# Low weights for all 128 rows in the last matmul of each spatial group

## The chip, the cores and the metric

The kernel runs on one core of a Trainium2 chip. The metric is device time in microseconds (us) of one execution on that core. Three runs were timed; the median counts.

## What is computed

The reference chains three blocks in float32: a causal windowed attention (4 batches, 8 heads, 576 positions, head size 64), a mixing block with a hidden layer of 2048, and a gated block. The change lies in the last one:

```python
h = np.maximum(x @ w_in, 0.0)
u, v = (h[..., :d_ff // 2], h[..., d_ff // 2:])
mu = np.mean(v, axis=-1, keepdims=True)
var = np.mean((v - mu) ** 2, axis=-1, keepdims=True)
v_n = (v - mu) / np.sqrt(var + 1e-06)
v_s = np.einsum('ts,bsd->btd', w_spatial, v_n) + b_spatial[None, :, None]
gated = u * v_s
return (gated @ w_out).astype(np.float32)
```

Here `x` is 4 x 576 x 512, `h` has 1024 columns (512 for `u`, 512 for `v`) and `w_spatial` is 576 x 576. The product with `w_spatial` runs over the 576 positions `s`.

## The kernel before

All matmuls of the two later blocks take float32 operands split in two: a high part that TensorE (PE) reads as float32r, and a low part, the float32 value less the high part. A product a·b is summed from three matmuls: high·high, high·low and low·high. ScalarE (ACT) makes a high part by a copy, GpSimd (POOL) or VectorE (DVE) the low part by a subtraction.

The order of every engine's work comes from a planner (class `Plan`). Each operation is added with an engine, an estimated cost, what it reads and writes, and a priority; `run` simulates the engines with these costs and emits the operations in the order in which they would start. So a changed cost or an added operation can reorder other work on any engine.

The gated block goes batch by batch (`b` = 0 to 3), in three stages each, with one more between:

- `values_of` multiplies by the v half of `w_in`, for chunks of 128 positions, and normalises each position. Per chunk DVE gets mean and variance, POOL the power -1/2 (tile `rs`, L831), DVE the normalised values (L833), ACT the high part (L848) and DVE the low part (L851).
- `outputs_of` of the batch before multiplies by `w_out`.
- `gates_of` first makes the u half (its matmuls are recorded at L779 to L781, those of the helper `triple`), then the **spatial product**.

576 positions are 64 + 4 x 128. The four chunks of 128 (`c` = 1 to 4) have separate tiles for high and low. The first 64 positions (`c` = 0) are packed: in one tile of 128 partitions, one half of the rows holds the high part and the other half the low part of the same 64 positions. For even batches the high part is in rows 0 to 63, for odd batches in rows 64 to 127 (L841 and L843 write the two halves; slice `hi` in `gates_of` names the half with the high part). The transposed spatial weights `ws[0]` of these 64 positions are therefore loaded twice, into both halves of a tile; `ws[c][:, 0]` is the high and `ws[c][:, 1]` the low part (L759 ACT, L761 POOL).

For each batch the spatial product has 8 groups: 4 blocks of 128 columns times 2 halves of 288 positions. One group is 14 matmuls into one PSUM tile (function `spatial`, L881 to L891):

- for each of the four chunks three matmuls, L886 high·high, L887 high·low, L888 low·high, each 128 rows by 288 columns;
- L890: the packed tile against the high weights in all 128 rows, which gives high·high and low·high together;
- L891: the packed tile against the low weights, in the 64 rows of the high part alone.

After a group DVE adds the bias (L897) and multiplies by the u half (L899), ACT takes high parts (L910) and POOL low parts (L912). The groups' results go to eight PSUM tiles in turn (names `acc`, `sc`, `f`, `at`).

Of the kernel before, what the change touches and what calls it, by code (L numbers as in the profile page):

```python
# [11 lines left out]
F32 = mybir.dt.float32  # L12
F32R = mybir.dt.float32r
# [3 lines left out]
ALU = mybir.AluOpType  # L17
PSUM = bass.MemoryType.PSUM

B, H, S, D = 4, 8, 576, 64  # L20
# [45 lines left out]
def f32(ap):  # L66
    return ap.bitcast(F32)
# [171 lines left out]
def mm(n, m=128):  # L239
    return (max(n, 2 * m) + m / 4) / 2400  # L240


def dve(n):
    return n / 960 + 0.066
# [6 lines left out]
def act(n, src=0.06, aps=0):  # L251
    return n / 1200 + src + 0.09 * aps


def pool_tt(n):
    return 0.0021 * n + 0.15
# [3 lines left out]
def tile_kernel(ctx, tc, qT, kT, v, U, V, w1, w2, w_in, wspT, bsp, w_out, bias, out):  # L260
    nc = tc.nc
    ctx.enter_context(nc.allow_low_precision("operands split exactly into float32r parts"))
    P = Plan()
# [432 lines left out]
    for pair in range(4):  # L696
        P.dma(128, 192, lambda pair=pair: nc.sync.dma_start(out=bias_t[:, pair], in_=bias[:, pair]),
              w=[bias_t.part(pair)], prio=20 * pair + 0.5)
# [24 lines left out]
    def late(tag, n):  # L723
        return Ring(late_pool, tag, n, [end_att])
# [6 lines left out]
    base = 2e4  # L731
# [19 lines left out]
    ws = []  # L751
    for c, (s0, n) in enumerate(CH):
        st = r_raw.new([128, S], F32)

        b_ = (r_wb if c < 4 else r_raw).new([128, 2, S], F32R)
        for p0 in (0, 64) if c == 0 else (0,):
            P.dma(n, S, lambda st=st, p0=p0, s0=s0, n=n: nc.sync.dma_start(
                out=st[p0 : p0 + n], in_=wspT[s0 : s0 + n, :]), w=[st], prio=base - 900)
        P.add("ACT", act(S, 0.09), lambda st=st, b_=b_: nc.scalar.copy(out=b_[:, 0], in_=st.ap()),  # L759
              r=[st], w=[b_.part(0)], prio=base - 900)  # L760
        P.add("POOL", pool_tt(S), lambda st=st, b_=b_: nc.gpsimd.tensor_tensor(  # L761
            out=b_[:, 1], in0=st.ap(), in1=f32(b_[:, 0]), op=ALU.subtract), r=[st, b_.part(0)], w=[b_.part(1)], prio=base - 900)
        ws.append(b_)
    bb = late("bb", 1).new([128, S], F32)
    P.dma(128, S, lambda: nc.sync.dma_start(
        out=bb.ap(), in_=bsp.rearrange("(o s) -> o s", o=1).broadcast_to([128, S])), w=[bb], prio=base - 1000)
# [5 lines left out]
    def next_ps(shape):  # L772
        turn[0] += 1
        return pss[turn[0] % 8].new(shape, F32)

    def triple(o, pairs):

        for i, (lh, ll, rh, rl) in enumerate(pairs):
            nc.tensor.matmul(o, lh, rh, start=i == 0, stop=False)  # L779
            nc.tensor.matmul(o, lh, rl, start=False, stop=False)  # L780
            nc.tensor.matmul(o, ll, rh, start=False, stop=i == len(pairs) - 1)  # L781

    def halves(w):
        return [w.part(0), w.part(1)]
# [71 lines left out]
    def gates_of(b, base):  # L856
        yh, yl, vn = stage[b]
        u2 = []
        for f in range(4):
            fs = slice(f * 128, f * 128 + 128)  # L860
            t = (r_y if b < 3 else r_y3).new([128, S], F32)
            for s0 in (0, 288):
                sl = slice(s0, s0 + 288)
                o = next_ps([128, 288])
                P.add("PE", 12 * mm(288), lambda o=o, sl=sl, fs=fs: triple(o.ap(), [
                    (win_u[k][:, 0, 0, fs], win_u[k][:, 1, 0, fs], yh[k][:, sl], yl[k][:, sl]) for k in range(4)]),
                    r=yh + yl + [p for w in win_u for p in halves(w)], w=[o], prio=base)
                P.add("ACT", act(288), lambda o=o, t=t, sl=sl: nc.scalar.activation(out=t[:, sl], in_=o.ap(), func=AF.Relu),
                      r=[o], w=[t.part(s0)], prio=base)
            u2.append(t)  # L870
        hi = slice(b % 2 * 64, b % 2 * 64 + 64)
        if b % 2 == 0:
            stage[b, 1] = stage[b + 1, 1] = r_wa.new([128, 2, 4, 128], F32R)
        gm = stage[b, 1]
        gh, gl = [], []
        for f in range(4):
            fs = slice(f * 128, f * 128 + 128)
            h_, l_ = r_u.new([128, S], F32R), r_u.new([128, S], F32R)
            for s0 in (0, 288):
                sl = slice(s0, s0 + 288)  # L880
                o = next_ps([128, 288])  # L881

                def spatial(o=o, fs=fs, sl=sl):
                    for c in range(1, 5):
                        a, l = vn[c]
                        nc.tensor.matmul(o.ap(), a[:, fs], ws[c][:, 0, sl], start=c == 1, stop=False)  # L886
                        nc.tensor.matmul(o.ap(), a[:, fs], ws[c][:, 1, sl], start=False, stop=False)  # L887
                        nc.tensor.matmul(o.ap(), l[:, fs], ws[c][:, 0, sl], start=False, stop=False)  # L888
                    t = vn[0][0]
                    nc.tensor.matmul(o.ap(), t[:, fs], ws[0][:, 0, sl], start=False, stop=False)  # L890
                    nc.tensor.matmul(o.ap(), t[hi, fs], ws[0][hi, 1, sl], start=False, stop=True)  # L891

                P.add("PE", 14 * mm(288), spatial,
                      r=[p for a, l in vn for p in (a.part(0), l.part(1))] + [p for w in ws for p in halves(w)],
                      w=[o], prio=base + 1)
                g = r_st.new([128, 288], F32)
                P.add("DVE", dve(288), lambda o=o, g=g, sl=sl: nc.vector.tensor_tensor(  # L897
                    out=g.ap(), in0=o.ap(), in1=bb[:, sl], op=ALU.add), r=[o, bb], w=[g], prio=base + 1)
                P.add("DVE", dve(288), lambda g=g, f=f, sl=sl: nc.vector.tensor_tensor(  # L899
                    out=g.ap(), in0=g.ap(), in1=u2[f][:, sl], op=ALU.mult), r=[u2[f].part(s0)], w=[g], port=True, prio=base + 1)  # L900
                regions = [(slice(0, 288), lambda h_=h_: h_[:, 288:], lambda l_=l_: l_[:, 288:], h_.part(288), l_.part(288))]
                if s0 == 0:
                    regions = [
                        (slice(0, 64), lambda f=f: gm[:, 0, f, hi], lambda f=f: gm[:, 1, f, hi],
                         gm.part((0, f, b % 2)), gm.part((1, f, b % 2))),
                        (slice(64, 288), lambda h_=h_: h_[:, 64:288], lambda l_=l_: l_[:, 64:288], h_.part(0), l_.part(0)),
                    ]
                for cs, oh, ol, ph, pl in regions:
                    n = cs.stop - cs.start
                    P.add("ACT", act(n, 0.09), lambda g=g, oh=oh, cs=cs: nc.scalar.copy(out=oh(), in_=g[:, cs]),  # L910
                          r=[g], w=[ph], prio=base + 1)
                    P.add("POOL", pool_tt(n), lambda g=g, oh=oh, ol=ol, cs=cs: nc.gpsimd.tensor_tensor(  # L912
                        out=ol(), in0=g[:, cs], in1=f32(oh()), op=ALU.subtract), r=[g, ph], w=[pl], prio=base + 1)
            gh.append(h_)
            gl.append(l_)
        stage[b] = (gh, gl, gm)
# [26 lines left out]
    for b in range(B):  # L943
        values_of(b, base + 100 * b)
        if b:
            outputs_of(b - 1, base + 100 * b + 5)
        gates_of(b, base + 100 * b + 10)
# [49 lines left out]
```

## Time and profile before

| | us |
|---|---|
| median of 3 runs | 777.17 |
| lowest, highest run | 774.2, 777.43 |
| span of the profiled execution | 773.6 |
| PE busy in that span | 748.1 (97%) |

The page gives no total for the profiled execution beside its span, so the span is its own time here; it lies 0.6 us under the lowest run and 3.6 us under the median. Mean granted TensorE clock over the span: 0.990 of full speed. In the rows further down, times are us from the span's start, PE is the matmuls, PEld the weight loads that precede each matmul, and a bracket holds the idle time of the engine just before the instruction, with what ended it.

### The profile page before, as it was taken

The numbers are of one execution on the slowest core, as the hardware profiler recorded it, in microseconds if no ns is written. First come the engines' busy times: TensorE is split into PE (matmuls) and PEld (weight loads), VectorE is DVE, ScalarE is ACT, GpSimd is POOL, SyncE is SP. The second block draws the span as 40 slices with busy tenths as digits, with TensorE's granted clock in tenths as the row PEclk, the third lists the DMA queues.
The fourth block names the chain that finished last, engine by engine and source line by source line (L and its number), as shares of the span: only waits on it lengthen the run. The fifth ranks groups of instructions, "written<-read, shape, count | busy, mean of one in ns | idle before, by whom it ended". The sixth has DMA issues, their size and how long they took to land.

```text
span 773.6 us, 13053 instructions
## 1 busy us (share of the span) xinstructions
PE 748.1 (97%) x4988; PEld 635.7 (82%) x4988; DVE 414.4 (54%) x1077; ACT 317.7 (41%) x856; POOL 263.7 (34%) x344
## 2 busy tenths in 40 slices
PE   6788999999899999999999999999999999999998
PEld 5566878889677888898888888888898898898987
DVE  5989677576699832237952272222845325325120
ACT  6767566574445422124531242321552332332322
POOL 1253231110655642125861253530555043043021
PEclk9989999999999999999999999999999999999999
DMA  7846213120605100024000110001300100200102
GB/s 216 278 153 187 63 42 114 35 76 1 219 15 175 43 1 1 1 83 134 1 1 0 60 51 1 0 1 50 105 1 1 55 1 1 69 1 1 55 1 68
DMA packets 28834, 45.70 MB, mean 59 GB/s; under 512 B 4964, under 2 KB 18020, under 8 KB 28772
## 3 DMA queue, kind: packets, MB, share of 16 engines
q1 hardware_dynamic: 28772, 44.87, 18.3%
q8 instruction: 39, 0.64, 0.3%
q14 instruction: 23, 0.19, 0.1%
HBM read 40.14 MB, written 4.72 MB: 58 GB/s over the span
## 4 chain that ended last, share of the span: by engine, by line
PE 87%; DVE 9%; ACT 2%; issue 1%; DMA 1%; SPq 0%; POOL 0%; ACTq 0%; DVEq 0%; POOLq 0%
PE sc L497 5%; PE sc L498 5%; PE sc L499 5%; PE at L460 5%; PE at L461 5%; PE at L462 5%; PE at L616 4%; PE at L639 3%; PE acc L497 3%; PE acc L499 3%; PE acc L498 3%; PE f L460 3%; PE at L780 3%; PE at L779 3%; PE at L781 3%; PE f L461 3%
## 5 line engine op out<-in xcount | busy, mean ns | idle before, releaser
L434 POOL TENSOR_TENSOR x<-u,xc 128x64 fp32r<-128x64 f32 (+5 forms) x108 | 92.8, 893 | 134.3 <-ACT xc L431 133.0
L469 DVE SCALAR_TENSOR_TENSOR h<-at,h 128x512 fp32r<-128x512 f32 (+1 forms) x51 | 32.7, 641 | 96.5 <-ACT h L467 96.5
L467 ACT ACTIVATE h<-at 128x512 fp32r<-128x512 f32 (+1 forms) x51 | 28.6, 560 | 125.9 <-PE at L462 125.8
L594 ACT ACTIVATE p<-p,nmax 128x192 f32<-128x192 f32 (+1 forms) x144 | 61.4, 430 | 9.4 <-DVE nmax L589 9.3
L616 PE MATMUL at<-ident,p 128*128 128x128 f32 x272 | 41.6, 296 | 6.2 <-DVE p L609 5.0
L589 DVE CUSTOM_DVE_ANT_0 p<-sc,bias 128x192 f32<-128x192 f32 (+1 forms) x144 | 39.8, 326 | 14.0 <-PE sc L577 13.9
L460 PE MATMUL at<-xc,wb 128*128 128x512 f32 (+1 forms) x120 | 44.2, 368 | 0.0
L497 PE MATMUL sc<-h,wb 128*128 128x512 f32 (+1 forms) x120 | 44.2, 368 | 0.0
L499 PE MATMUL sc<-h,wb 128*128 128x512 f32 (+1 forms) x120 | 44.1, 368 | 0.0
L498 PE MATMUL sc<-h,wb 128*128 128x512 f32 (+1 forms) x120 | 44.1, 368 | 0.0
L462 PE MATMUL at<-x,wb 128*128 128x512 f32 (+1 forms) x120 | 44.1, 368 | 0.0
L461 PE MATMUL at<-xc,wb 128*128 128x512 f32 (+1 forms) x120 | 44.1, 368 | 0.0
L577 PE MATMUL sc<-kr,qr 64*64 64x192 f32 (+2 forms) x576 | 33.5, 332 | 10.7 <-DMA kr<-in_kT 6.7
L616 PEld LDWEIGHTS at<-ident,p 128*128 128x128 f32 x272 | 33.0, 150 | 12.7 <-issue 4.2
L384 POOL TENSOR_TENSOR wa<-st,wa 128x512 fp32r<-128x512 f32 x24 | 32.6, 1367 | 31.4 <-ACT wa L317 27.8
L794 POOL TENSOR_TENSOR u<-y,u 128x576 fp32r<-128x576 f32 x16 | 23.1, 1459 | 55.6 <-ACT u L792 55.6
L384 POOL TENSOR_TENSOR wb<-st,wb 128x512 fp32r<-128x512 f32 x20 | 30.9, 1555 | 31.3 <-ACT wb L317 31.3
L469 DVE SCALAR_TENSOR_TENSOR h<-f,h 128x512 fp32r<-128x512 f32 (+1 forms) x27 | 17.8, 658 | 43.0 <-ACT h L467 42.9
L431 ACT CAST xc<-u 128x64 fp32r<-128x64 f32 (+5 forms) x108 | 38.3, 437 | 3.8 <-PE at L687 3.8
L467 ACT ACTIVATE h<-f 128x512 fp32r<-128x512 f32 (+1 forms) x27 | 15.4, 571 | 53.2 <-PE f L462 52.1
L497 PE MATMUL acc<-h,wa 128*128 128x256 f32 (+1 forms) x108 | 35.6, 329 | 1.5 <-DVE y L507 1.2
L577 PEld LDWEIGHTS sc<-kr,qr 64*64 64x64 f32 x576 | 21.8, 141 | 17.5 <-issue 10.1
(323 smaller groups left out, 2279.2 us busy)
## 6 DMA issues: line engine op xcount, KB each, us to landing
wa<-in_w SPq DMA_DIRECT2D x16, 512.0 KB, 4.9
wb<-in_w SPq DMA_DIRECT2D x16, 512.0 KB, 5.6
qr<-in_qT SPq DMA_DIRECT2D x16, 288.0 KB, 2.9
kr<-in_kT SPq DMA_DIRECT2D x16, 288.0 KB, 3.8
vr<-in_v SPq DMA_DIRECT2D x16, 256.0 KB, 2.8
wa<-in_w_in SPq DMA_DIRECT2D x8, 512.0 KB, 3.5
out<-h SPq DMA_DIRECT2D x15, 256.0 KB, 2.0
wb<-in_w_out SPq DMA_DIRECT2D x4, 512.0 KB, 4.0
```

Of the source, the lines that this page charges most:

```text
L384: P.add("POOL", pool_tt(k * c), lambda: nc.gpsimd.tensor_tensor(out=b[:, 1], in0=st.ap(), in1=f32(b[:, 0]), op=ALU.subtract), r=[st, b.par ...
L434: nc.gpsimd.tensor_tensor(out=tl[il][:, o : o + m], in0=ub[:, s : s + m], in1=f32(th[ih][:, o : o + m]), op=ALU.subtract)
L460: nc.tensor.matmul(o, wt[:, 0, k], a[ia], start=k == 0, stop=False)
L461: nc.tensor.matmul(o, wt[:, 1, k], a[ia], start=False, stop=False)
L462: nc.tensor.matmul(o, wt[:, 0, k], l[il], start=False, stop=k == 3)
L469: P.add("DVE", dve(per * n), lambda f1=f1, hh=hh, hl=hl: nc.vector.scalar_tensor_tensor(out=hl.ap(), in0=f1.ap(), scalar=0.0, in1=f32(hh.a ...
L497: nc.tensor.matmul(o, wt[:, 0, 0, c], hh[:, j], start=i == 0 and x == 0, stop=False, skip_group_check=True)
L498: nc.tensor.matmul(o, wt[:, 1, 0, c], hh[:, j], start=False, stop=False, skip_group_check=True)
L499: nc.tensor.matmul(o, wt[:, 0, 0, c], hl[:, j], start=False, stop=i == len(wts) - 1, skip_group_check=True)
L577: nc.tensor.matmul(s[o : o + 64, c0 : c0 + k1 - k0], qr[d, 64 * t : 64 * t + 64], kr[d, k0:k1], start=True, stop=True, skip_group_check=True)
L594: nc.scalar.activation(out=o(), in_=o(), func=AF.Exp, scale=-1.0, bias=nmax[:, sl, t : t + 1], accum_out=sums[:, sl, t : t + 1])
L616: P.add("PE", 0.109, lambda pt=pt, t=t, half=half, blk=blk: nc.tensor.transpose(pt[:, blk * 128 : blk * 128 + 128], p[:, t, half * 128 : h ...
```

## The change

The last matmul of a group, L891, took 64 rows of the packed tile and the same 64 rows of the low weights. It now takes all 128 rows of the packed tile, against low weights whose other 64 rows are zero. Since the half with the high part alternates with the batch, there are two such tiles: `ws[0][:, 1]` (low weights in rows 0 to 63, zeros below) for even batches and the new tile `wz` (zeros above, low weights in rows 64 to 127) for odd ones. POOL makes each with a subtraction in 64 rows and a memset in the other 64. The sum that a group computes is the same.

```diff
-        P.add("POOL", pool_tt(S), lambda st=st, b_=b_: nc.gpsimd.tensor_tensor(
-            out=b_[:, 1], in0=st.ap(), in1=f32(b_[:, 0]), op=ALU.subtract), r=[st, b_.part(0)], w=[b_.part(1)], prio=base - 900)
+        if c == 0:
+
+            wz = late("wz", 1).new([128, S], F32R)
+            for i, to in enumerate((lambda b_=b_: b_[:, 1], wz.ap)):
+                lo, no = slice(64 * i, 64 * i + 64), slice(64 - 64 * i, 128 - 64 * i)
+                part = (b_, wz)[i].part(1)
+                P.add("POOL", pool_tt(S), lambda st=st, b_=b_, to=to, lo=lo: nc.gpsimd.tensor_tensor(
+                    out=to()[lo], in0=st[lo], in1=f32(b_[lo, 0]), op=ALU.subtract), r=[st, b_.part(0)], w=[part], prio=base - 900)
+                P.add("POOL", 0.5, lambda to=to, no=no: nc.gpsimd.memset(to()[no].bitcast(F32), 0.0), w=[part], prio=base - 900)
+        else:
+            P.add("POOL", pool_tt(S), lambda st=st, b_=b_: nc.gpsimd.tensor_tensor(
+                out=b_[:, 1], in0=st.ap(), in1=f32(b_[:, 0]), op=ALU.subtract), r=[st, b_.part(0)], w=[b_.part(1)], prio=base - 900)
...
-                    nc.tensor.matmul(o.ap(), t[hi, fs], ws[0][hi, 1, sl], start=False, stop=True)
+                    nc.tensor.matmul(o.ap(), t[:, fs], wz[:, sl] if b % 2 else ws[0][:, 1, sl], start=False, stop=True)
...
-                      r=[p for a, l in vn for p in (a.part(0), l.part(1))] + [p for w in ws for p in halves(w)],
+                      r=[p for a, l in vn for p in (a.part(0), l.part(1))] + [p for w in ws for p in halves(w)] + [wz.part(1)],
```

In the changed kernel the lines behind the first hunk stand ten further down: L831 is L841, L843 is L853, L886 to L891 are L896 to L901.

POOL's order just ahead of the first spatial product, before (`st` and `raw` are staged weights of `w_out` and `w_spatial`, `rs` the power -1/2 of a chunk):

```order
L384 TENSOR_TENSOR wb<-st,wb 128x512
L761 TENSOR_TENSOR wb<-raw,wb 128x576
L384 TENSOR_TENSOR wb<-st,wb 128x512
L761 TENSOR_TENSOR wb<-raw,wb 128x576 x2
L384 TENSOR_TENSOR wb<-st,wb 128x512
L831 TENSOR_TENSOR rs<-rs,half 128x1
L761 TENSOR_TENSOR wb<-raw,wb 128x576
L384 TENSOR_TENSOR wb<-st,wb 128x512
L761 TENSOR_TENSOR raw<-raw 128x576
L831 TENSOR_TENSOR rs<-rs,half 128x1 x4
```

and at the same place of the changed kernel:

```order
L384 TENSOR_TENSOR wb<-st,wb 128x512
L767 TENSOR_TENSOR wb<-raw,wb 64x576
L769 MEMSET wb 64x576
L767 TENSOR_TENSOR wz<-raw,wb 64x576
L771 TENSOR_TENSOR wb<-raw,wb 128x576
L769 MEMSET wz 64x576
L384 TENSOR_TENSOR wb<-st,wb 128x512
L771 TENSOR_TENSOR wb<-raw,wb 128x576 x2
L384 TENSOR_TENSOR wb<-st,wb 128x512 x2
L841 TENSOR_TENSOR rs<-rs,half 128x1 x2
L771 TENSOR_TENSOR raw<-raw 128x576
L841 TENSOR_TENSOR rs<-rs,half 128x1 x3
```

One subtraction has become two and two memsets have come in; the planner has moved the first `rs` behind the last two of the four `w_out` subtractions. DVE and ACT are reordered in the same stretch; SP's queue is not.

PE keeps its order throughout. Around the end of the first group of batch 1 it reads before (names with their numbers; `wb_5856` is `ws[0]`, `xc_6144` the packed tile):

```order
L886 MATMUL sc_6675<-raw_6031,x_6521 128x288
L887 MATMUL sc_6675<-raw_6031,x_6521 128x288
L888 MATMUL sc_6675<-raw_6031,xc_6523 128x288 [waits DVE_49]
L890 MATMUL sc_6675<-wb_5856,xc_6144 128x288
L891 MATMUL sc_6675<-wb_5856,xc_6144 128x288
L886 MATMUL sc_6699<-wb_5913,x_6439 128x288 [waits Activation_49]
```

and in the changed kernel:

```order
L896 MATMUL sc_6679<-raw_6049,x_6525 128x288
L897 MATMUL sc_6679<-raw_6049,x_6525 128x288
L898 MATMUL sc_6679<-raw_6049,xc_6527 128x288 [waits DVE_49]
L900 MATMUL sc_6679<-wb_5856,xc_6165 128x288
L901 MATMUL sc_6679<-wz_5905,xc_6165 128x288
L896 MATMUL sc_6703<-wb_5915,x_6443 128x288 [waits Activation_49]
```

Only the weights of the last matmul of the group are another tile, and no wait is added (the size printed is that of the result, so the rows that are summed over do not show).

## Rows read from the trace of the kernel before

**Rows 1.** The page: busy time of each engine, and the chain that ended last.
```profile
PE 748.1 (97%) x4988; PEld 635.7 (82%) x4988; DVE 414.4 (54%) x1077; ACT 317.7 (41%) x856; POOL 263.7 (34%) x344
...
PE 87%; DVE 9%; ACT 2%; issue 1%; DMA 1%; SPq 0%; POOL 0%; ACTq 0%; DVEq 0%; POOLq 0%
```

**Rows 2.** Windows over the four spatial products (two shown): length, busy (count), clock, DMA share, GB/s.
```profile
core 0: us, PE busy (x) PEld busy (x) DVE busy (x) ACT busy (x) POOL busy (x), PEclk, DMA share, GB/s
...
628.26:646.14 17.88, 17.88 (x114) 15.43 (x112) 9.00 (x14) 6.10 (x16) 12.02 (x15) 1.00 0.01 1
686.21:704.04 17.83, 17.83 (x114) 15.39 (x112) 9.10 (x14) 6.21 (x16) 11.94 (x15) 1.00 0.00 1
...
sum 71.41, PE 71.41 PEld 61.62 DVE 33.10 ACT 22.34 POOL 41.98; mean PE 17.85 PEld 15.40 DVE 8.28 ACT 5.59 POOL 10.50
```

**Rows 3.** Timeline of PE, first group of batch 0 into the second: start, duration, operation.
```profile
575.80 0.29 PE L886 MATMUL sc<-wb,x 128*128 128x288 f32 x1
...
577.38 0.29 PE L890 MATMUL sc<-wb,x 128*128 128x288 f32 x1
577.61 0.39 PE L891 MATMUL sc<-wb,x 64*128 64x288 f32 x1
577.93 0.40 PE L886 MATMUL sc<-wb,x 128*128 128x288 f32 x1
578.17 0.30 PE L887 MATMUL sc<-wb,x 128*128 128x288 f32 x1
578.31 0.29 PE L888 MATMUL sc<-wb,xc 128*128 128x288 f32 x1
```

**Rows 4.** Timeline of the weight loads in the same place.
```profile
577.61 0.18 PEld L891 LDWEIGHTS sc<-wb,x 64*128 64x128 f32 x1 [0.16 <-issue]
577.93 0.19 PEld L886 LDWEIGHTS sc<-wb,x 128*128 128x128 f32 x1
578.04 0.19 PEld L887 LDWEIGHTS sc<-wb,x 128*128 128x128 f32 x1
```

**Rows 5.** All instructions of line L891: idle time ahead of them, by releaser, with count.
```profile
  issue: 5.2, 32
```

**Rows 6.** Timeline of PE where a group of 128-row matmuls ends and the next begins.
```profile
572.49 0.30 PE L781 MATMUL at<-u,wa 128*128 128x288 f32 x1
572.63 0.29 PE L779 MATMUL acc<-u,wa 128*128 128x288 f32 x1
```

**Rows 7.** Timeline of POOL ahead of the first spatial product.
```profile
546.36 1.71 POOL L761 TENSOR_TENSOR wb<-raw,wb 128x576 fp32r<-128x576 f32 x1 [0.25 <-ACT wb L759]
551.26 1.31 POOL L384 TENSOR_TENSOR wb<-st,wb 128x512 fp32r<-128x512 f32 x1 [3.20 <-ACT wb L317]
...
559.09 1.51 POOL L761 TENSOR_TENSOR wb<-raw,wb 128x576 fp32r<-128x576 f32 x1 [1.14 <-ACT wb L759]
...
562.27 1.43 POOL L761 TENSOR_TENSOR raw<-raw 128x576 fp32r<-128x576 f32 x1
```

**Rows 8.** Groups of POOL's memsets over the whole span: busy us, mean ns.
```profile
L560 POOL MEMSET v<- 64x128 f32 x16 | 3.3, 210 | 52.2 <-issue 26.4 <-PE at L639 25.8
L533 POOL MEMSET p<- 128x256 f32 x4 | 1.1, 312 | 0.0
L533 POOL MEMSET p<- 128x64 f32 x4 | 0.5, 152 | 0.0
```

**Rows 9.** Timeline of DVE: the last operand of the first spatial product.
```profile
570.43 0.69 DVE L843 TENSOR_TENSOR xc<-h,xc 64x512 fp32r<-64x512 f32 x1
```

**Rows 10.** Timeline of POOL at the end of the last spatial product.
```profile
755.71 0.32 POOL L912 TENSOR_TENSOR wa<-st,wa 128x64 fp32r<-128x64 f32 x1 [1.25 <-ACT wa L910]
```

**Rows 11.** Timeline of PE from the end of the last spatial product.
```profile
756.47 0.50 PE L779 MATMUL f<-wb,wa 128*128 128x512 f32 x1
756.81 0.39 PE L780 MATMUL f<-wb,wa 128*128 128x512 f32 x1
757.04 0.39 PE L781 MATMUL f<-wb,wa 128*128 128x512 f32 x1
```

## The prediction

> **What bounds the kernel now.** I read the page first: PE is busy for 97% of the span and makes up 87% of the chain that ended last [rows 1]. So time is saved only where PE gets through its own list faster, and work of the other engines counts only where PE would come to wait for it. Next, the windows over the four spatial products [rows 2]: each lasts 17.83 to 17.88 us, PE is busy from end to end, and the granted clock is 1.00, the upper of its two levels (2.4 GHz). POOL has at most 12.02 us of work in such a window, DVE 9.10, ACT 6.21.
>
> "Busy" hides what matters, since matmuls overlap. The quantity to read is the distance from one start to the next. In the timeline of PE [rows 3] the first 13 matmuls of a group start between 575.80 and 577.38, 12 distances in 1.58 us, or 0.132 us each. Then comes the last matmul, L891, over 64 rows. It starts 0.23 us after L890, the next group's first matmul 0.32 us after it, and that group's second another 0.24 us later. From there the distance is 0.14 again. The loads tell why [rows 4]: the load of an ordinary matmul starts 0.13 us before its matmul (L887, 578.04 against 578.17), while the one ahead is still running. The 64-row load starts with its own matmul at 577.61, after 0.16 us of idle time that nothing else explains ("issue"). The 128-row load after it, at 577.93, again starts only with its matmul. So a change in the number of rows, in either direction, costs the overlap of load and matmul. It is no single event: all 32 executions of L891 (4 batches of 8 groups) have that idle time, 5.2 us in all [rows 5].
>
> **The change part by part.** *The last matmul takes 128 rows.* The columns stay 288, and as many matmuls and loads are issued as before, in the same order. What goes is the two switches. Three distances from L890 to the second matmul of what follows are now 578.17 - 577.38 = 0.79 us; three ordinary ones would be 3 x 0.132 = 0.396. That saves 0.394 us per group, and 32 x 0.394 = **12.6 us**. A second way to the same sum: the four windows add up to 71.41 us [rows 2]; 4 x 112 = 448 matmuls at 0.132 are 59.1; the difference of 12.3 and four times the 0.1 us by which the last group delays the stage after its window give 12.7.
>
> The bounds of this saving: the last of the three distances, 0.24 against 0.132, is the one least surely tied to the switch. If it stayed, the saving would be 0.55 - 0.26 = 0.29 per group, 9.3 us. The upper end reads the ordinary distance as 0.13: 448 of them are 58.2 us, and the second sum gives 71.41 + 0.4 - 58.2 = 13.6 us. I take 12.6, since a 128-row matmul behind another one, at the end of a group and into another PSUM tile, starts 0.14 us after it [rows 6].
>
> The rule that speaks against this is in the Trainium skill, page "TensorE: Matmul & The Clock Gate", section "Part 3: Packing small matmuls — row/col tiling": it says that a weight load overlaps a running matmul only when the two use different row groups. By it, a 128-row load behind a 128-row matmul could not go ahead either, and the saving would be 0. The trace disagrees here: L887's load starts at 578.04, 0.11 us into L886's 0.40 us, with the same 128 rows [rows 3, 4].
>
> *POOL's preparation.* One subtraction over 128x576 (1.71 us [rows 7]) becomes two over 64x576, plus two memsets of 64x576. No row shows a POOL subtraction over 64 partitions; the bounds are half of 1.43 us, were time to follow the rows, and 1.71. I take 1.71, because the memsets do not follow the rows: 64x128 takes 0.210 us, between 0.152 for 128x64 and 0.312 for 128x256 [rows 8]. By the last two, one column more costs 0.00083 us, so 576 columns make an estimated 0.58 us; the ends are 0.31 (the longest memset shown) and 0.95 (4.5 times 0.210). Added in all: 1.71 + 2 x 0.58 = 2.9 us, between 0.3 and 3.6. Two things hide it. POOL idles 3.20 and 1.14 us in this stretch, 4.3 together, waiting for ACT [rows 7]. So little or none of it should reach the `rs` behind. If that cover is gone, the next one holds: the last operand of the first spatial product is ready at 570.43 + 0.69 = 571.12 [rows 9], and PE starts that product at 575.80, after the u half, 4.7 us later. The last low weights are ready at 562.27 + 1.43 = 563.7. I cost it at **0**. With both covers gone it is 3.6 us at most, once.
>
> *The reordering.* `rs` of the first chunk goes behind two `w_out` subtractions, which delays only chunk values with the same 4.7 us to spare. DVE and ACT change places within the same stretch: **0**. SP's queue is as before: 0.
>
> *What a faster PE meets.* A spatial window shrinks to 112 x 0.132 = 14.8 us; POOL's 12.0 us still fit. At the very end PE goes from the last spatial product straight to the outputs of batch 3, whose first chunk needs what POOL finishes at 755.71 + 0.32 = 756.03 [rows 10]. PE arrives at 756.47 [rows 11], 0.44 us later. PE will come some 0.4 us earlier in relation to that, so this slack is used up. But the part still being written is read only by the fourth of its four steps, 9 matmuls at 0.23 us or more (2.1 us) further on: **0**.
>
> **The sum.** 773.6 - 12.6 = 761.0 for the span. The profiled execution lies 3.6 us under the median of the runs; a saving on PE is the same for all of them, so the median becomes 777.17 - 12.6 = **764.5 us** (1.6% less).
>
> **The rivals.** *Part of the distances stays.* If the slow distances belong partly to the end of a group, not to the rows, for example to the packed tile being loaded twice in a row, a remainder is left. If only the idle time at the load goes (5.2 us), the result is 772.0. Against it: L886 and L887 also load the same tile twice, and are among the 12 distances of 0.132.
>
> *The load stays behind.* The gap is a matter of the place in the program, and no load is pulled ahead whatever its rows: 777.2, no change. For it: every slow load in these stages stands at this one place. Against it: the ordinary group end, without a gap [rows 6]. The rule named above would come to the same time.
>
> *POOL's list becomes the wait* (slower). The `rs` of the first chunks now stand behind all four `w_out` subtractions. Should POOL be held up there by the transfers or by DVE, normalised values come late and PE stands still before the first spatial product. It begins to cost at a delay of 4.7 us; it eats the whole gain at 17.3, and the kernel is slower by over 0.5% from 21.2 us, 781.1 us. For it: the planner did move this work. Against it: the idle times there are 3.20 and 1.14 us, and the added work is 3.6 us at most.
>
> **How the numbers follow.** Forecast (all three distances ordinary) 0.91; part of them stays 0.04; the load stays behind 0.03; POOL's list 0.02. A measurement of this kernel can tell about 0.5%, 3.9 us, from no change: below 773.3 is faster. The first two cases are faster, 0.95; the third is the same, 0.03; the last slower, 0.02. The range takes the bounds of the saving and the spread of the runs: low is the lowest run less the upper bound, 774.2 - 13.6 = 760.6; high is 777.17 - 9.3 = 767.9, rounded to 768.0. It leaves out the rivals, 9 in 100, and some of the scatter.
>
> **What would show it.** Right: in the changed trace the idle time ahead of L901's loads is near 0 instead of 5.2 us, its duration is near 0.29 instead of 0.39 us, L900 to the second matmul behind L901 takes 0.40 us, and a spatial window 14.8 us; PE does not wait ahead of the first spatial product, and the last DVE operand still ends before PE wants it. Wrong: a distance of over 0.2 us around L901, or PE idle between 560 and 580 us or at the start of the last outputs.

## The result, and the profile after

| | before | changed |
|---|---|---|
| median, us | 776.92 (4 runs, 774.2 to 777.43) | 763.40 (4 runs, 761.83 to 763.91) |
| span of the profiled execution, us | 773.6 | 762.1 |

The ratio is 0.9834, 95% interval [0.9814, 0.9855]: the kernel is faster by 1.7%, 13.5 us by the medians (the kernel before was run once more, which moved its median from 777.17 to 776.92). The forecast was 764.5, with 12.6 us saved. In a later comparison on one chip, with 23 runs of the kernel before and 6 of the changed one, the medians are 776.02 and 763.26, 12.8 us apart.

The spans differ by 11.5 us, the medians by 13.5. In every run that has both numbers on record the time is 1.7 to 1.9 us longer than the span, so the span of 773.6 stands for a time near 775.4, which is 1.5 us under the median of its kernel, while 762.1 belongs to the run of 763.91, 0.5 us over the median of its own.

The page of the changed kernel is much as before [rows 1]: PE is still what the chain runs through.

```profile
PE 735.4 (96%) x4988; PEld 633.0 (83%) x4988; DVE 414.4 (54%) x1077; ACT 318.5 (42%) x856; POOL 268.4 (35%) x347
...
PE 87%; DVE 9%; ACT 1%; DMA 1%; issue 1%; SPq 0%; POOL 0%; ACTq 0%; DVEq 0%; POOLq 0%
```

PE has as many matmuls as before (4988) and 12.7 us less busy time. POOL has three instructions more and 4.7 us more; 3.1 us of that are the preparation (worked out below), and most of the rest stands at operations that are the same in both kernels (those of the line that is L912 before and L922 now, over 128x288, went from 13.3 to 14.3 us). Why those took longer is not shown.

The timeline of PE around the end of the first group of batch 0, which answers to [rows 3] (start, duration, operation):

```profile
578.41 0.29 PE L900 MATMUL sc<-wb,x 128*128 128x288 f32 x1
578.55 0.29 PE L901 MATMUL sc<-wb,x 128*128 128x288 f32 x1
578.68 0.30 PE L896 MATMUL sc<-wb,x 128*128 128x288 f32 x1
578.82 0.29 PE L897 MATMUL sc<-wb,x 128*128 128x288 f32 x1
```

The distances 0.23, 0.32 and 0.24 us have become 0.14, 0.13 and 0.14. The three take 0.41 us in place of 0.79. The loads in the same place (against [rows 4]):

```profile
578.42 0.19 PEld L901 LDWEIGHTS sc<-wb,x 128*128 128x128 f32 x1
578.55 0.19 PEld L896 LDWEIGHTS sc<-wb,x 128*128 128x128 f32 x1
578.68 0.19 PEld L897 LDWEIGHTS sc<-wb,x 128*128 128x128 f32 x1
```

Each load now starts 0.13 us ahead of its own matmul, while the matmul before it runs. (What L901 loads is 128 columns of the packed tile; the low weights are its 288 columns.) In the summary of line L901 the entry "issue: 5.2, 32" [rows 5] is gone, and the matmul's duration has fallen from 0.39 to 0.29 us:

```profile
L901 PE MATMUL sc<-wb,x x6: 292/294/295, 578.5 to 695.6; 128*128 128x288 f32 x6
...
its engine sat idle before it (us, times) until:
who waited for it (us, times):
```

The windows over the four spatial products (against [rows 2]; length, busy time and count by engine, clock, DMA share, GB/s):

```profile
576.83:591.69 14.86, 14.86 (x115) 14.86 (x113) 8.50 (x14) 6.19 (x16) 11.93 (x14) 1.00 0.01 1
626.19:640.99 14.80, 14.80 (x114) 14.80 (x113) 7.95 (x14) 6.10 (x16) 11.97 (x14) 1.00 0.00 1
680.91:695.76 14.85, 14.85 (x114) 14.85 (x113) 8.23 (x14) 6.19 (x16) 11.93 (x14) 1.00 0.01 1
730.25:745.09 14.84, 14.84 (x114) 14.84 (x113) 6.41 (x14) 3.83 (x12) 5.63 (x11) 1.00 0.00 1
sum 59.35, PE 59.35 PEld 59.35 DVE 31.09 ACT 22.30 POOL 41.46; mean PE 14.84 PEld 14.84 DVE 7.77 ACT 5.58 POOL 10.37
```

The sum fell from 71.41 to 59.35, by 12.1 us, and the load engine, which stood idle for one us in every seven, is now busy from end to end. The spans differ by less, 11.5 us, since the first spatial product starts 1.03 us later than before (576.83 against 575.80). From that start to the end of the span it is 773.6 - 575.80 = 197.8 us before and 762.1 - 576.83 = 185.3 after: 12.5 less.

### The profile page after: what moved, and what is told of

Read it like the earlier page. It is cut to its first block, busy times and chain, and to the rows that moved or that the text cites. A ratio compares the mean times of both kernels' runs of the same rounds, so it can differ in the third digit from the quotient of the medians.

```text
span 762.1 us, 13056 instructions
## 1 busy us (share of the span) xinstructions
PE 735.4 (96%) x4988; PEld 633.0 (83%) x4988; DVE 414.4 (54%) x1077; ACT 318.5 (42%) x856; POOL 268.4 (35%) x347
## 4 chain that ended last, share of the span: by engine, by line
PE 87%; DVE 9%; ACT 1%; DMA 1%; issue 1%; SPq 0%; POOL 0%; ACTq 0%; DVEq 0%; POOLq 0%
PE sc L497 5%; PE sc L499 5%; PE sc L498 5%; PE at L460 5%; PE at L462 5%; PE at L461 5%; PE at L616 4%; PE acc L497 3%; PE at L639 3%; PE acc L499 3%; PE acc L498 3%; PE f L460 3%; PE at L791 3%; PE at L790 3%; PE at L789 3%; PE f L461 3%
## 5 line engine op out<-in xcount | busy, mean ns | idle before, releaser
L577 PE MATMUL sc<-kr,qr 64*64 64x192 f32 (+2 forms) x576 | 34.3, 335 | 11.9 <-DMA kr<-in_kT 4.6
L577 PEld LDWEIGHTS sc<-kr,qr 64*64 64x64 f32 x576 | 22.1, 141 | 19.1 <-issue 15.7
```

Of the source, the lines that this page charges most:

```text
L577: nc.tensor.matmul(s[o : o + 64, c0 : c0 + k1 - k0], qr[d, 64 * t : 64 * t + 64], kr[d, k0:k1], start=True, stop=True, skip_group_check=True)
```

## The experiments

**One edit, without the preparation.** `ws[0][:, 1]` of the kernel before already has the low weights in both halves, so the last matmul can take all 128 rows with no zeros and no second tile:

```diff
-                    nc.tensor.matmul(o.ap(), t[hi, fs], ws[0][hi, 1, sl], start=False, stop=True)
+                    nc.tensor.matmul(o.ap(), t[:, fs], ws[0][:, 1, sl], start=False, stop=True)
```

> The kernel before with one edit: the last matmul of each group takes all 128 rows against the low weights that stand in both halves already, without zeros and without the second tile; so it also adds the product of the two low parts, which the kernel before leaves out. POOL's work and every engine's order stay those of before. Theory (the change of row count is the whole cost, POOL's preparation is hidden): as the changed kernel, 763.4 us, within 1.5. Rival (the preparation costs something after all): below the changed kernel by up to 3.6 us, about 760. Rival (zeros in the operand matter): no gain, 776.9.

Measured: 763.69 us against 776.02 of the kernel before on the same chip; ratio 0.9845 [0.982, 0.987]. Beside it on the same chip the changed kernel once more:

> The changed kernel once more, on the same chip as the other three, so that differences below one per cent can be read. All theories: 763.4 us, within 1.5.

Measured: 763.26 us; ratio 0.9851 [0.9823, 0.988]. The two cannot be told apart, and the entry of 5.2 us of idle time ahead of the loads of L891 is gone in this trace too. The whole gain comes with the row count of one matmul; zeros are not needed for it.

**The preparation alone.** The changed kernel, its last matmul put back to 64 rows:

```diff
-                    nc.tensor.matmul(o.ap(), t[:, fs], wz[:, sl] if b % 2 else ws[0][:, 1, sl], start=False, stop=True)
+                    nc.tensor.matmul(o.ap(), t[hi, fs], wz[hi, sl] if b % 2 else ws[0][hi, 1, sl], start=False, stop=True)
```

> The changed kernel with its last matmul put back to 64 rows, so only the added work of POOL, the second tile and the planner's new order are left. Theory (all of this is hidden): as before, 776.9 us, within 1.5. Rival (the list of POOL costs time that the gain has covered): 778 to 780.5.

Measured: 776.31 us against 776.02; ratio 1.0005 [0.9983, 1.0028]. POOL's extra work and the planner's new order cost nothing that can be measured (the interval leaves room for 2.2 us), and all the idle time ahead of the 64-row loads is back, to the digit of [rows 5]:

```profile
  issue: 5.2, 32
```

**The 64-row matmul moved.** In the kernel before, it goes from the end of a group to behind the second chunk; the full packed product then ends the group:

```diff
+                        if c == 2:
+                            nc.tensor.matmul(o.ap(), t[hi, fs], ws[0][hi, 1, sl], start=False, stop=False)
...
-                    nc.tensor.matmul(o.ap(), t[:, fs], ws[0][:, 0, sl], start=False, stop=False)
-                    nc.tensor.matmul(o.ap(), t[hi, fs], ws[0][hi, 1, sl], start=False, stop=True)
+                    nc.tensor.matmul(o.ap(), t[:, fs], ws[0][:, 0, sl], start=False, stop=True)
```

> The kernel before with the 64-row matmul of each group moved from the end to the middle, behind the second chunk. Theory (each change of row count costs, wherever it stands): as before, 776.9 us, within 2, and the three long distances of 0.23, 0.32 and 0.24 us now stand around the moved matmul, with ordinary 0.13 at the group's end. Rival (the place is what costs: the end of a group, the second use of the packed tile): most of the gain without more rows, 764 to 770.

Measured: 775.67 us against 776.02; ratio 1.0001 [0.9982, 1.002]. The timeline of PE, in the middle of the first group and at its end (L892 is the full packed product):

```profile
577.64 0.29 PE L889 MATMUL sc<-wb,xc 128*128 128x288 f32 x1
577.87 0.40 PE L891 MATMUL sc<-wb,x 64*128 64x288 f32 x1
578.20 0.40 PE L887 MATMUL sc<-wb,x 128*128 128x288 f32 x1
578.43 0.29 PE L888 MATMUL sc<-wb,x 128*128 128x288 f32 x1
...
579.09 0.29 PE L892 MATMUL sc<-wb,x 128*128 128x288 f32 x1
579.22 0.30 PE L887 MATMUL sc<-wb,x 128*128 128x288 f32 x1
```

The distances 0.23, 0.33 and 0.23 have moved along with the matmul, and the group's end has an ordinary 0.13. The rival that blamed the place falls.

**Two of them side by side.** Call a change between 64 and 128 rows, from one matmul to the next, a *switch*; the spatial products of the kernel before have 64 of them, one into and one out of each 64-row matmul. Every second group of the kernel before begins with its 64-row matmul, next to the one that ends the group ahead:

```diff
+                    first = s0 == 288
+                    if first:
+                        nc.tensor.matmul(o.ap(), t[hi, fs], ws[0][hi, 1, sl], start=True, stop=False)
...
-                    nc.tensor.matmul(o.ap(), t[hi, fs], ws[0][hi, 1, sl], start=False, stop=True)
+                    if not first:
+                        nc.tensor.matmul(o.ap(), t[hi, fs], ws[0][hi, 1, sl], start=False, stop=True)
```

> The kernel before with the 64-row matmul put first in every second group, so that two of them stand next to each other at 16 places and the row count changes 32 times in place of 64. Theory (the change of row count costs, 0.394 us for one way in and one way out): half the loss is gone, 776.9 - 16 x 0.394 = 770.6 us, within 1.5, and the distance between the two neighbours is ordinary, near 0.13. Rival (each 64-row matmul is slow by itself, its load never goes ahead): 776.9, with over 0.2 us between the two.

Measured: 769.88 us against 775.55; ratio 0.993 [0.9907, 0.9954], so 5.7 us are gone, near the half of 12.6 that was expected. One detail was expected otherwise, and it is the one that the rival foretold: over 0.2 us between the two neighbours. The timeline of PE at such a pair (L893 the full packed product, L895 and L887 the pair):

```profile
580.19 0.29 PE L893 MATMUL sc<-wb,x 128*128 128x288 f32 x1
580.41 0.40 PE L895 MATMUL sc<-wb,x 64*128 64x288 f32 x1
580.65 0.29 PE L887 MATMUL sc<-wb,x 64*128 64x288 f32 x1
580.87 0.40 PE L890 MATMUL sc<-wb,x 128*128 128x288 f32 x1
581.11 0.30 PE L891 MATMUL sc<-wb,x 128*128 128x288 f32 x1
581.24 0.29 PE L892 MATMUL sc<-wb,xc 128*128 128x288 f32 x1
```

and its loads:

```profile
580.41 0.18 PEld L895 LDWEIGHTS sc<-wb,x 64*128 64x128 f32 x1 [0.16 <-issue]
580.52 0.19 PEld L887 LDWEIGHTS sc<-wb,x 64*128 64x128 f32 x1
580.87 0.19 PEld L890 LDWEIGHTS sc<-wb,x 128*128 128x128 f32 x1 [0.16 <-issue]
```

The distance between the neighbours is 0.24, not 0.13. Yet the second 64-row load goes ahead (580.52, 0.13 us before its matmul), and that matmul takes the ordinary 0.29 us. So a 64-row matmul is not slow by itself. The 0.24 belongs to the switch ahead: it stands behind the first matmul after a switch (the one that starts together with its load and is printed with 0.40 us), both where that one and the next have 64 rows (580.41 to 580.65) and where both have 128 (580.87 to 581.11). Here the two switches stand apart, and one can be read alone: 0.22 and 0.24 in place of twice 0.132, a loss of 0.09 + 0.11 = 0.20 us. In the kernel before, the two overlap in the middle distance, 0.32 = 0.132 + 0.11 + 0.09 but for rounding.

**96 rows.** The kernel before with 96 rows in even batches and 128 in odd ones:

```diff
-                    nc.tensor.matmul(o.ap(), t[hi, fs], ws[0][hi, 1, sl], start=False, stop=True)
+                    n = 128 if b % 2 else 96
+                    nc.tensor.matmul(o.ap(), t[:n, fs], ws[0][:n, 1, sl], start=False, stop=True)
```

> The kernel before with the last matmul of each group over 96 rows in even batches and 128 rows in odd ones, against the low weights that stand in both halves; it also adds some or all of the product of the two low parts. If any number of rows below 128 counts as a change: the 16 groups of the even batches keep the loss, 763.4 + 16 x 0.394 = 769.7 us, within 1.5. If 96 rows go as 128 do and only the 64-row form is another: 763.4, within 1.5. I hold the second for the likelier, 0.6 to 0.4.

Measured: 763.95 us against 775.55; ratio 0.9841 [0.9814, 0.9868], which leaves out the 0.992 of the first case (half of 12.6 us saved: 769.25 / 775.55). The timeline of PE in batch 0:

```profile
579.53 0.29 PE L890 MATMUL sc<-wb,x 128*128 128x288 f32 x1
579.66 0.30 PE L892 MATMUL sc<-wb,x 96*128 96x288 f32 x1
579.80 0.29 PE L886 MATMUL sc<-wb,x 128*128 128x288 f32 x1
579.93 0.29 PE L887 MATMUL sc<-wb,x 128*128 128x288 f32 x1
```

The distances are ordinary. Fewer rows than 128 do not cost by themselves: 96 go as 128 do, 64 do not.

**The switches doubled.** The 64-row matmul of the kernel before is cut into two of 144 columns, one behind the second chunk, one at the end:

```diff
+                        if c == 2:
+                            nc.tensor.matmul(o[:, :144], t[hi, fs], ws[0][hi, 1, s0 : s0 + 144], start=False, stop=False)
...
-                    nc.tensor.matmul(o.ap(), t[hi, fs], ws[0][hi, 1, sl], start=False, stop=True)
+                    nc.tensor.matmul(o[:, 144:], t[hi, fs], ws[0][hi, 1, s0 + 144 : s0 + 288], start=False, stop=True)
```

> The kernel before with the 64-row matmul of each group cut into two of 144 columns, one behind the second chunk and one at the end, so the row count changes 128 times in place of 64 while the columns stay the same. Theory (cost per change): 776.9 + 12.6 and some 0.3 for 32 more matmuls, 789.8 us, within 2. Rival (the loss belongs to the columns or to the group's end): 777 to 778.5.

Measured: 788.90 us against 775.55; ratio 1.0169 [1.0141, 1.0196], 13.4 us slower. The columns are the same, the switches twice as many, and there are 32 more matmuls, for which the expectation put some 0.3 us. At the end of the first group:

```profile
578.50 0.29 PE L892 MATMUL sc<-wb,x 128*128 128x288 f32 x1
578.73 0.33 PE L893 MATMUL sc<-wb,x 64*128 64x144 f32 x1
578.99 0.40 PE L887 MATMUL sc<-wb,x 128*128 128x288 f32 x1
579.23 0.30 PE L888 MATMUL sc<-wb,x 128*128 128x288 f32 x1
```

With 144 columns the middle distance is 0.26 in place of 0.32, which is what 144 columns less make (by the ordinary distances, 0.132 us for 288 columns and 0.23 for 512 [rows 11], a column takes an estimated 0.0004 us, so 144 take 0.06); the two outer ones stay 0.23 and 0.24. Against the kernel before on the same chip each time, 64 switches less save 12.8 us, 32 less save 5.7, and 64 more cost 13.4, or 13.1 without the 0.3. That is 0.20, 0.18 and 0.20 us for each; the interval of the second, 0.11 to 0.23, holds the other two.

## Why the prediction was right

*The main term.* The three distances were to fall to 0.396 us and fell to 0.41; against the 12.6 us of the sum, the stretch from the first spatial product to the end lost 12.5 us, and the medians with most runs differ by 12.8. So the size was right by its mechanism. (That the profiled execution lies 3.6 us under the median is half a matter of measure: some 1.8 us of it are the difference of time and span that every run has. The saving does not depend on it.) The lower bound of the saving rested on the doubt that the last distance, 0.24, belongs to the switch; it is 0.14 in the changed kernel, it moved along with the 64-row matmul, and in the pair it stands behind each switch. Fewer switches save and more cost the same price for each, so it is shown that the switches are the cause, not only how much they cost.

One step of the reasoning was too wide. That "a change in the number of rows, in either direction, costs the overlap of load and matmul" holds for 128 to 64 and back; between 128 and 96 nothing is lost. The forecast needed the first alone.

*The rule against it.* The sentence of the Trainium skill, page "TensorE: Matmul & The Clock Gate", section "Part 3: Packing small matmuls — row/col tiling", that a load overlaps a running matmul only when their row groups differ, fails twice more: 128-row loads go ahead of their matmuls while other 128-row matmuls run in all four spatial products of the changed kernel (PEld is busy for 59.35 of 59.35 us), and the second of two neighbouring 64-row loads over the same rows goes ahead at 580.52. Another page of the Trainium skill fits: "TensorEngine Tiling (Array Packing)", section "Tiling Modes", names among its key properties that a change of the tiling mode drains TensorE, and its list has modes of 128, 64 and 32 rows, but none of 96. In these runs neighbours of 128 rows, and neighbours of 64, keep the overlap, each change between the two loses it, and 96 rows behave as 128. That the engine is emptied inside is the word of the Trainium skill; the rows show only that the load stops going ahead.

*POOL's preparation.* The cost was put at 0, and none is seen (ratio 1.0005 for the preparation alone). The reason given was right in one half. Here is POOL ahead of the first spatial product in the changed kernel:

```profile
547.39 1.83 POOL L767 TENSOR_TENSOR wb<-raw,wb 64x576 fp32r<-64x576 f32 x1
549.25 0.77 POOL L769 MEMSET wb<- 64x576 f32 x1
550.08 1.65 POOL L767 TENSOR_TENSOR wz<-raw,wb 64x576 fp32r<-64x576 f32 x1
552.93 1.43 POOL L771 TENSOR_TENSOR wb<-raw,wb 128x576 fp32r<-128x576 f32 x1 [1.20 <-ACT wb L759]
554.29 0.57 POOL L769 MEMSET wz<- 64x576 f32 x1
...
558.37 3.25 POOL L771 TENSOR_TENSOR wb<-raw,wb 128x576 fp32r<-128x576 f32 x2 [2.25 <-ACT wb L759]
561.58 3.00 POOL L384 TENSOR_TENSOR wb<-st,wb 128x512 fp32r<-128x512 f32 x2
564.53 1.19 POOL L841 TENSOR_TENSOR rs<-rs,half 128x1 f32<-128x1 f32 x2
```

The sizes held: two memsets of 0.77 and 0.57 us against an estimate of 0.58, and subtractions over 64 partitions of 1.83 and 1.65, which follow the columns and not the rows. Added in all are 1.83 + 0.77 + 1.65 + 0.57 - 1.71 = 3.1 us, against 2.9. But "little or none of it should reach the `rs` behind" failed. The idle time of 4.3 us that was to take it up did not vanish: 1.20 and 2.25 us of waiting for ACT are still in the list. With the planner's new order the first `rs` starts at 564.53, where it was 557.21 before. The last operand of the first spatial product comes later with it:

```profile
573.92 0.69 DVE L853 TENSOR_TENSOR xc<-h,xc 64x512 fp32r<-64x512 f32 x1
```

It is ready at 574.61, 2.2 us before PE starts the product at 576.83, where it was 4.7 us before [rows 9]. So the second cover carried the cost: 2.5 of its 4.7 us are used up. This is no scatter: in all six profiles with the order of before the slack is 4.7 us, in all three with the new order 2.2. The rival in which POOL's list becomes the wait had a real mechanism, and half its way to costing anything was gone. That the term came out right is owed to the second cover, not to the first.

*The end of the last product.* As worked out, the slack of 0.44 us [rows 10] is gone, and nothing waits:

```profile
744.80 0.33 POOL L922 TENSOR_TENSOR wa<-st,wa 128x64 fp32r<-128x64 f32 x1 [0.85 <-ACT wa L920]
```

```profile
745.09 0.40 PE L789 MATMUL f<-wb,wa 128*128 128x512 f32 x1
745.33 0.39 PE L790 MATMUL f<-wb,wa 128*128 128x512 f32 x1
```

POOL is done at 745.13, 0.04 us after PE has begun the outputs, but the matmul that needs this part comes nine matmuls later.

*The 1.03 us.* That the first spatial product starts later in the profiled execution is within the scatter and needs no cause in the change: the changed kernel profiled once more has that start at 575.37, and it was at 576.83 the first time; in the six profiles with the order of before it lies between 575.46 and 578.61. What scatters in the stages ahead of it is not shown.

## What to carry to other kernels

On PE read the distances between starts and the place of each load, not the busy time: a matmul over half the rows between matmuls over all of them cost two switches of 0.2 us each here, together as much as three ordinary matmuls of 288 columns. If it can't be avoided, fill its rows, or put such matmuls next to each other. Filling need not mean zeros: here the other half of the weights held the same numbers, and the product that this adds, low times low, belongs to the exact result, so a one-line edit gave the whole gain with no preparation and no second tile.

The changed kernel still has such places in the attention, where 64x64 matmuls (L577) stand between matmuls over 128 rows. The loads at one of them:

```profile
150.63 0.19 PEld L499 LDWEIGHTS acc<-h,wa 128*128 128x128 f32 x1
150.95 0.75 PEld L577 LDWEIGHTS sc<-kr,qr 64*64 64x64 f32 x24
151.98 0.19 PEld L497 LDWEIGHTS acc<-h,wa 128*128 128x128 f32 x1 [0.28 <-issue]
```

The 128-row matmuls there, over 256 columns, start 0.12 us apart; the step into the 64-row ones is 0.21 us (150.75 to 150.96), and the step behind the first 128-row matmul after them 0.23 (151.98 to 152.21). That is 0.09 and 0.11 us more, as in the spatial product. It is no clean test, since these loads have 64 columns in place of 128 too, and no run changed them. Nor does any run here try 32 rows or another number format.

## What was not expected

A switch shows in two distances, 0.09 us where the load comes late and 0.11 us behind that matmul, so half of its price stands at an instruction that looks ordinary. On POOL the first `rs` came over 6 us later in relation to PE, though the added work is 3.1 us, and half of the slack ahead of the first spatial product went. Less of a surprise, but open until measured (0.6 to 0.4): 96 rows cost no switch beside 128 (distances of 0.13 and 0.14 us), while 64 do.
